# Reordering a fused attention and mixture-of-depths kernel: square sums and PV ahead of the tail scores, transposes between the last two score blocks, gates spread by broadcast weights

## The chip, the core and the metric

The kernel runs on one core of a Trainium2 chip, alone. The metric is the device time of one execution in microseconds. Before the change it was 286.28 us, the median of three (286.19 to 293.61).

## The reference, cut to what matters

Cosine attention over 8 batches, 12 heads, 448 tokens of 64 elements, then a mixture-of-depths block in which the 128 best tokens of each batch pass through a two-layer network:

```python
q_n = q / (norm(q) + 1e-06);  k_n = k / (norm(k) + 1e-06)
attn = softmax(q_n @ k_n.T / tau)          # 448 x 448 for each head
x = attn @ v                               # -> [8, 448, 768]
scores = einsum('bsd,d->bs', x, w_gate)
for b in range(8):
    top_idx = argpartition(-scores[b], 128)[:128]
    h = maximum(x[b, top_idx] @ w1, 0)     # 768 -> 1024
    ye = h @ w2                            # 1024 -> 768
    out[b] = x[b]
    out[b, top_idx] += sigmoid(scores[b, top_idx])[:, None] * ye
```

## The kernel before

The loop runs over 48 pairs of heads, six to a batch. In iteration i, pair i gets its scores and exponentials, pair i - 1 its product with v (PV), pair i + 1 its transposes, pair i + 2 its scaling, and pair i + 6 its squares. 448 tokens are three chunks of 128 and a tail of 64; the tails of both heads of a pair share one block, `scores(i, 3)`. The norms are taken in groups: ScalarE squares, TensorE sums groups of eight with identity weights, VectorE finishes the sum, ScalarE takes the root (`norm_a`), VectorE the reciprocal (`norm_b`). The MoE block of a batch is spread in pieces over the iterations of the next batches; the letters D1, A, C, D3, B, P1 and P2 are the places in an iteration at which such pieces are issued.

```python
# ... pools, loads, constants; ps_sc: two buffers of two PSUM banks, in rotation; ps_t (qkT_ps), ps_o (o_ps), ps_m (m_ps): one buffer each ...
# ... square(p): squares of q and k of pair p on ScalarE; sum_pe(p): 8 matmuls with the identity add them by eights ...
def sum_dve(p, dst):
    n, m = nplace[p]
    nc.vector.tensor_reduce(
        ss_tiles[n][:, m].rearrange("p a b -> p (a b)"),
        dst.rearrange("p (n d) -> p n d", d=D8), axis=AX.X, op=ALU.add)

def norm_a(n):
    gn = NORMS[n][1]
    rs = prep.tile([P, 3, 2, NB7], FP32, name="rs", bufs=3)
    rs_tiles[n] = rs
    nc.scalar.activation(rs[:, :gn], ss_tiles[n][:, :gn], AF.Ln)
    nc.scalar.activation(rs[:, :gn], rs[:, :gn], AF.Exp, scale=0.5)
    nc.scalar.activation(rs[:, :gn], rs[:, :gn], AF.Identity, bias=epsb[:, 0:1])

def norm_b(n):
    gn = NORMS[n][1]
    r = rs_tiles[n][:, :gn].rearrange("p g a b -> p (g a b)")
    nc.vector.reciprocal(r, r)
# ... scale(p): q, k times rs to bf16 (qkn, one buffer) on GpSimd; values(p): v to bf16 on GpSimd;
# transposes(p): 28 PE transposes of qkn into qkT_ps; qkT_copy(p): VectorE copies them to SBUF ...
def scores(i, c, sc=None):
    qkT = qkT_tiles[i]
    if sc is None:
        sc = ps_sc.tile([P, 2, 512], FP32, name="sc")
    sc_tiles[i, c] = sc
    if c < NC:
        for u in range(2):
            r = slice(u * Dh, u * Dh + Dh)
            nc.tensor.matmul(out=sc[:, u, :S],
                             lhsT=qkT[r, KO + c * P:KO + (c + 1) * P],
                             rhs=qkT[r, :S], start=True, stop=True,
                             tile_position=(u * Dh, 0))
    else:
        nc.tensor.matmul(out=sc[:, 0, :S], lhsT=qkT[:, KT:W],
                         rhs=qkT[:, :S], start=True, stop=True)

# ... exps(i, c): exp of block c to bf16 in expS; pv_tails(i), pv(i): 8 + 24 matmuls of expS with vo into o_ps ...
# ... pv_evac(i), VectorE: rden = 1 / the sums in o_ps (L336), then o_ps times rden into x_b or, for the last pair, x_last (L338) ...
# ... store_x(b): DMA x_b -> out; half_x(b): DMA x_b -> xh in bf16; gate, rank_prep, bank, rank_rep: in the diff below;
# rank_count(b, j), pick(b, j): rank by counting and one-hot picks of 128 tokens, VectorE;
# select (8 matmuls), gather (24), ffn1 (2 x 24), ffn2 (2 x 8), scatter: the MoE block of batch b;
# at(slot, where, fn) queues MoE work for an iteration and a place, run(i, where) emits it ...
for i in range(N + 1):
    live, prev, nxt = i < N, i > 0, i + 1 < N
    # ... loads ...
    run(i, "P1")
    sq = SQ.get(i - 1, [])
    scores(i, 0)
    if prev:
        pv_tails(i - 1)
    sc = ps_sc.tile([P, 2, 512], FP32, name="sc")
    scores(i, 3, sc)
    sums(sq, sc)
    exps(i, 0)
    exps(i, 3)
    for p in SQ.get(i, []):
        square(p)
    run(i, "D1")
    sums_dve(sq, sc)
    norms(sq, i, True)
    if prev:
        pv(i - 1)
        pv_evac(i - 1)
    run(i, "A")
    if i < 3:
        warm(8)
    scores(i, 1)
    exps(i, 1)
    scores(i, 2)
    exps(i, 2)
    if nxt:
        transposes(i + 1)
        qkT_copy(i + 1)
    if i + 2 < N:
        scale(i + 2)
        values(i + 2)
    run(i, "P2")
    run(i, "C")
    norms(sq, i, False)
    run(i, "D3")
    if i < 3:
        warm(8)
    run(i, "B")

# ... after the loop: PV of the last pair, the rest of batch 6, all of batch 7 (in the diff) ...
```

## Time and profile before

One profiled execution, span 286.9 us, mean granted TensorE clock 0.957. All times below are from it.

| part of the work | where | each |
|---|---|---|
| exponentials of a full block, 128x896 | L293, ScalarE, 144 times | 914 ns |
| exponentials of a tail block, 128x448 | L296, ScalarE, 48 times | 538 ns |
| squares, 128x896 | L197, ScalarE, 48 times | 945 ns |
| last step of the square sums | L210, VectorE, 48 times | 272 ns |
| gate product of a chunk, 128x768 | L358, VectorE, 28 times | 1103 ns |
| rank by counting, 128x448 | L408, VectorE, 24 times | 677 ns |
| gates on a diagonal, 128x512 | L366, GpSimd, 7 times | 1076 ns |
| gates spread by fp32 product, 128x448 | L396, TensorE, 16 records | 587 ns |
| scaling of q and k, 128x896 | L235, GpSimd, 47 times | 1689 ns |

The profile's page gives the busy time of each engine, the costliest groups of instructions (line, engine, operation, output and inputs, number, busy time, mean of one) and the chain of work that ended last. PE is TensorE's matmuls, PEld its weight loads, DVE is VectorE, ACT ScalarE, POOL GpSimd. The view of waits has, for an engine and a line, what ended its idle time, how long in total, how often, and the longest. In the timeline a row is a start, a duration, the engine, the line and the operation, with the idle time before it in brackets.

57.55 MB are moved in all, 201 GB/s on the mean. Loads of q and k take about 10 us from issue to landing.

### The profile page before, as it was taken

The numbers are of one execution on the slowest core, as the hardware profiler recorded it, in microseconds if no ns is written. First come the engines' busy times: TensorE is split into PE (matmuls) and PEld (weight loads), VectorE is DVE, ScalarE is ACT, GpSimd is POOL, SyncE is SP. The second block draws the span as 40 slices with busy tenths as digits, with TensorE's granted clock in tenths as the row PEclk, the third lists the DMA queues.
The fourth block names the chain that finished last, engine by engine and source line by source line (L and its number), as shares of the span: only waits on it lengthen the run. The fifth ranks groups of instructions, "written<-read, shape, count | busy, mean of one in ns | idle before, by whom it ended". The sixth has DMA issues, their size and how long they took to land.

```text
span 286.9 us, 10402 instructions
## 1 busy us (share of the span) xinstructions
PE 230.8 (80%) x4503; PEld 174.2 (61%) x4503; DVE 181.3 (63%) x482; ACT 208.4 (73%) x322; POOL 150.7 (53%) x183
## 2 busy tenths in 40 slices
PE   7576687788599979997998869987799679859760
PEld 7365565566477657765875548755577457538540
DVE  2313336985776679667875497848866777795620
ACT  3677979999588798888896788869777665573310
POOL 6443465879345674567445747376348463902202
PEclk9997979999789999999799999999999999997997
DMA  7999999999999996999599969998704580549444
GB/s 266 284 252 286 263 263 249 315 276 260 261 309 293 273 193 150 285 273 210 113 247 287 252 112 217 283 270 153 177 21 88 82 194 3 105 61 184 104 55 55
DMA packets 32989, 57.55 MB, mean 201 GB/s; under 512 B 2224, under 2 KB 28784, under 8 KB 32048
## 3 DMA queue, kind: packets, MB, share of 16 engines
q1 hardware_dynamic: 28016, 43.75, 57.8%
q0 software_dynamic: 4512, 12.45, 24.5%
q8 instruction: 35, 0.57, 0.8%
q10 hardware_dynamic: 416, 0.69, 0.7%
q14 instruction: 10, 0.08, 0.1%
HBM read 39.71 MB, written 14.16 MB: 188 GB/s over the span
## 4 chain that ended last, share of the span: by engine, by line
PE 41%; DVE 21%; ACT 16%; DMA 10%; issue 7%; POOL 2%; SPq 1%; POOLq 1%; DVEq 0%; ACTq 0%
ACT expS L293 8%; PE sc L280 8%; DMA qk_raw<-in_k_dram 6%; PE o_ps L320 6%; PE m_ps L483 5%; DVE junk L408 5%; PE qkT_ps L262 5%; DVE junk L358 4%; DMA xh<-x_b 4%; PE sc L204 4%; PE m_ps L475 4%; ACT sq L197 3%; PE m_ps L462 3%; PE sc L285 3%; POOL qkn L235 2%
## 5 line engine op out<-in xcount | busy, mean ns | idle before, releaser
L293 ACT ACTIVATE expS<-sc 128x896 bf16<-128x896 f32 x144 | 126.5, 914 | 37.6 <-PE sc L280 36.8
L235 POOL TENSOR_TENSOR qkn<-qk_raw,rs 128x896 bf16<-128x896 f32 (+1 forms) x48 | 80.7, 1681 | 101.0 <-PE qkT_ps L262 44.0
L280 PE MATMUL sc<-qkT 64*128 64x448 bf16 x288 | 49.3, 368 | 28.8 <-DVE qkT L268 15.6
L197 ACT ACTIVATE sq<-qk_raw 128x896 bf16<-128x896 f32 x48 | 45.1, 945 | 6.0 <-DMA qk_raw<-in_k_dram 4.2
L320 PE MATMUL o_ps<-vo,expS 128*128 128x65 bf16 x1152 | 46.3, 197 | 0.0
L320 PEld LDWEIGHTS <-expS 128*128 128x128 bf16 x1152 | 42.7, 100 | 0.5
L280 PEld LDWEIGHTS <-qkT 64*128 64x128 bf16 x288 | 13.1, 94 | 45.4 <-issue 20.4
L268 DVE COPY qkT<-qkT_ps 128x960 bf16<-128x960 bf16 x48 | 31.4, 655 | 12.5 <-PE qkT_ps L262 12.5
L262 PEld LDWEIGHTS <-qkn 64*64 64x64 bf16 x1344 | 25.4, 111 | 15.8 <-issue 11.0
L338 DVE TENSOR_TENSOR x_b<-o_ps,rden 128x512 f32<-128x512 f32 x47 | 32.5, 691 | 2.3 <-DMA xh<-x_b 0.7
L358 DVE CUSTOM_DVE_ANT_0 junk<-x_b,wg_b 128x768 bf16<-128x768 f32 (+1 forms) x32 | 33.3, 1040 | 0.2
L262 PE MATMUL qkT_ps<-iden_b,qkn 64*64 64x64 bf16 x1344 | 30.8, 196 | 2.1 <-POOL qkn L235 2.1
L242 POOL CAST vo<-v_raw 128x448 bf16<-128x448 f32 x48 | 32.0, 668 | 0.0
L210 DVE TENSOR_REDUCE ss<-sc 128x14 f32<-128x112 f32 x48 | 12.7, 272 | 29.6 <-ACT expS L296 24.5
L296 ACT ACTIVATE expS<-sc 128x448 bf16<-128x448 f32 x48 | 25.8, 538 | 5.1 <-PE sc L204 5.1
L204 PE MATMUL sc<-sq,iden_b 128*128 128x112 bf16 x384 | 28.0, 222 | 0.0
L204 PEld LDWEIGHTS <-iden_b 128*128 128x128 bf16 x384 | 24.7, 103 | 4.9 <-issue 1.3
L475 PEld LDWEIGHTS <-w_sb 128*128 128x128 bf16 x384 | 22.3, 99 | 3.2 <-issue 2.2
L408 DVE SCALAR_TENSOR_TENSOR junk<-m_ps,own,tie 128x448 bf16<-128x448 f32 (+1 forms) x32 | 21.8, 680 | 0.9
L225 DVE RECIPROCAL rs<-rs 128x42 f32<-128x42 f32 (+2 forms) x18 | 7.0, 387 | 22.3 <-ACT rs L220 14.1
L498 POOL DMA_INDIRECT out_dram<-oe,idx x8 | 13.0, 1628 | 14.5 <-DVE oe L448 7.0
L475 PE MATMUL m_ps<-xeT,w_sb 128*128 128x128 bf16 x288 | 18.1, 219 | 1.6 <-DVE xeT L446 1.6
(90 smaller groups left out, 272.6 us busy)
## 6 DMA issues: line engine op xcount, KB each, us to landing
qk_raw<-in_q_dram SPq DMA_DIRECT2D x15, 672.0 KB, 9.8
qk_raw<-in_k_dram SPq DMA_DIRECT2D x15, 672.0 KB, 9.4
v_raw<-in_v_dram SPq DMA_DIRECT2D x30, 192.0 KB, 10.0
out_dram<-x_b SPq DMA_DIRECT2D x7, 768.0 KB
xh<-x_b POOLq DMA_DIRECT2D x7, 768.0 KB, 8.3
v_raw<-in_v_dram SPq DMA_DIRECT2D x30, 144.0 KB, 9.0
out_dram<-x_b SPq DMA_DIRECT2D x7, 576.0 KB, 4.7
w_sb<-in_moe_w_dram POOLq DMA_DIRECT2D x2, 1536.0 KB, 19.8
```

The costliest lines, as they stand in the source:

```text
L197: nc.scalar.activation(sq_tiles[p], raw[gi % NRAW][0][:, :, g].rearrange("p a b d -> p a (b d)"), AF.Square)
L204: nc.tensor.matmul(out=dst, lhsT=iden_b, rhs=sq[:, :, s * D8:(s + 1) * D8], start=(s == 0), stop=(s == Dh // D8 - 1))
L235: eng.tensor_mul(kn[:, :, b0:b1], qk[:, :, g, b0:b1], rs[:, m, :, b0:b1].rearrange("p a (b o) -> p a b o", o=1) .to_broadcast([P, 2, b1 - ...
L242: nc.gpsimd.tensor_copy(vo_bufs[p % NB][:, :, :Dh], raw[gi % NRAW][1][:, g])
L262: nc.tensor.transpose(out=qkT_ps[r, o:o + T], in_=kn[r, a, s], identity=iden_b[r, r], tile_position=(u * T, u * T))
L280: nc.tensor.matmul(out=sc[:, u, :S], lhsT=qkT[r, KO + c * P:KO + (c + 1) * P], rhs=qkT[r, :S], start=True, stop=True, tile_position=(u * D ...
L293: nc.scalar.activation(ex[:, 2 * c:2 * c + 2], sc[:, :, :S], AF.Exp, scale=inv_tau)
L320: nc.tensor.matmul(out=o_ps[:, u, j * E:(j + 1) * E], lhsT=ex[:, 2 * c + u, qc(j)], rhs=vo[:, u * NS + c], start=False, stop=(c == NC - 1) ...
L338: nc.vector.tensor_mul(dst.rearrange("p j (u d) -> p j u d", u=2), o[:, :, :, :Dh], rden.to_broadcast([P, NS, 2, Dh]))
L358: nc.vector.tensor_tensor_reduce(out=junk[:, d0:d1], in0=x_tiles[b][:, j, d0:d1], in1=wg_b[:, d0:d1], scale=1.0, scalar=0.0 if prev is Non ...
L408: nc.vector.scalar_tensor_tensor(out=junk[r], in0=st[b]["rep"][r, :S], scalar=st[b]["own"][r, j:j + 1], in1=tie[r, j, :], op0=ALU.subtract ...
L475: nc.tensor.matmul(out=ps[:, f * CAP:(f + 1) * CAP], lhsT=w1_sb[:, t, fc * P:(fc + 1) * P], rhs=xeT[t], start=(t == 0), stop=(t == KD - 1))
```

## The change

It changes the order within an iteration and does three things besides.

- **Order.** The square sums and the PV product of the pair before go ahead of the tail score block on TensorE; on VectorE the sums go ahead of the gates, with one rank count (the new place D0) in front. The transposes of the next pair go between score blocks 1 and 2, from pair 2 on. The reciprocal of a norm group moves to the next iteration. The purpose is that an engine's queue doesn't stand before a late input while ready work is behind it.
- **Places of the MoE pieces.** Gate products move by an iteration or to D3; the preparation of the ranks goes to a new place, P1b; squares of the first pairs move later; norm groups become aligned with the load groups.
- **Spreading the gates.** Each token's gate has to stand on all partitions. Before, GpSimd put the gates on a diagonal, and a product with ones in fp32 spread them. After, the gate is split into three bf16 parts (these existed already for the selection), and each part's column, broadcast to 128 columns, is the weight operand of a product with the identity: 15 small products in place of two fp32 ones.
- **The tail.** The score buffers are closed after the loop and four one-bank tiles opened in their place. The last batch's gates are reduced chunk by chunk, the last chunk's on GpSimd and ScalarE, the spreading is issued in the middle of an ffn1, and ffn1 and ffn2 are cut in two so that they can start on the first half of their input.

```diff
@@ -78,7 +79,7 @@
     starts = {g0: gi for gi, (g0, gn) in enumerate(GROUPS)}
     place = {g0 + g: (gi, g) for gi, (g0, gn) in enumerate(GROUPS) for g in range(gn)}
-    NORMS = [(0, 1), (1, 2), (3, 2)]
+    NORMS = [(0, 1), (1, 2), (3, 2), (5, 1)]
     while sum(NORMS[-1]) < N:
         NORMS.append((sum(NORMS[-1]), min(3, N - sum(NORMS[-1]))))
     nplace = {g0 + g: (n, g) for n, (g0, gn) in enumerate(NORMS) for g in range(gn)}
# ... iden_f, ones_f, iden_x and their fills: removed; ps_sc: opened last, so that it can be closed ...
@@ -351,53 +343,49 @@
# ... gate(b, j, d0, d1, prev, dst): sum of x * w_gate over columns d0 to d1 on VectorE (L358); gets x as another source ...
-    def rank_prep(b, split=False):
+    def rank_prep(b, eng=None):
         g = gates[b % 2]
-        diag = moe.tile([P, NS, P], FP32, name="diag", bufs=1)
-        nc.gpsimd.tensor_mul(
-            diag[:, :2 if split else NS], iden_x[:, :2 if split else NS],
-            g[:, :2 if split else NS].rearrange("p (j o) -> p j o", o=1)
-            .to_broadcast([P, 2 if split else NS, P]))
-        if split:
-            for j in (2, 3):
-                nc.scalar.activation(diag[:, j], iden_x[:, j], AF.Copy,
-                                     scale=g[:, j:j + 1])
+        eng = eng or nc.gpsimd
         sg = moe.tile([P, NS, 3], BF16, name="sg")
         r1 = moe.tile([P, NS], FP32, name="r1")
-        nc.gpsimd.tensor_copy(sg[:, :, 0], g)
-        nc.gpsimd.tensor_sub(r1, g, sg[:, :, 0])
-        nc.gpsimd.tensor_copy(sg[:, :, 1], r1)
-        nc.gpsimd.tensor_sub(r1, r1, sg[:, :, 1])
-        nc.gpsimd.tensor_copy(sg[:, :, 2], r1)
-        st[b].update(diag=diag, sg=sg)
+        eng.tensor_copy(sg[:, :, 0], g)
+        eng.tensor_sub(r1, g, sg[:, :, 0])
+        eng.tensor_copy(sg[:, :, 1], r1)
+        eng.tensor_sub(sg[:, :, 2], r1, sg[:, :, 1])
+        st[b]["sg"] = sg
     wide = []
     def bank(big=False):
         if not big:
             return ps_m.tile([P, 512], FP32, name="m_ps")
-        if not wide:
-            t = ps_sc.tile([P, 2, 512], FP32, name="sc")
-            wide.extend((t[:, 1], t[:, 0]))
-        return wide.pop()
+        return wide[0].tile([P, 512], FP32, name="w_ps")
     def rank_rep(b):
-        g, diag = gates[b % 2], st[b]["diag"]
+        sg = st[b]["sg"]
         rep = bank()
-        nc.tensor.matmul(out=rep[:, :S], lhsT=ones_f,
-                         rhs=diag.rearrange("p j c -> p (j c)")[:, :S],
-                         start=True, stop=True)
-        nc.tensor.matmul(out=rep[:, S:S + NS], lhsT=iden_f, rhs=g,
-                         start=True, stop=True)
+        for j in range(NS):
+            c0, n = (j * P, P) if j < NC else (SM, T)
+            for e in range(3):
+                nc.tensor.matmul(out=rep[:, c0:c0 + n],
+                                 lhsT=sg[:, j, e:e + 1].to_broadcast([P, P]),
+                                 rhs=iden_b[:, P - n:], start=(e == 0), stop=(e == 2))
+        for e in range(3):
+            nc.tensor.matmul(out=rep[:, S:S + NS], lhsT=iden_b, rhs=sg[:, :, e],
+                             start=(e == 0), stop=(e == 2))
         own = moe.tile([P, NS], FP32, name="own")
         nc.vector.tensor_copy(own, rep[:, S:S + NS])
         st[b].update(rep=rep, own=own)
@@ -464,17 +452,23 @@
                                  start=(j == 0), stop=(j == NS - 1))
         evac(eng, xe.rearrange("p t c -> p (t c)"), ps[:, :(t1 - t0) * CAP], AF.Copy)
-    def ffn1(b, part, eng="D", big=False):
+    def ffn1(b, part, eng="D", big=False, cut=0, between=None):
         xeT = st[b]["xeT"]
         h = moe.tile([P, 4, CAP], BF16, name=f"hT{part}")
         st[b].setdefault("hT", []).extend(h[:, t] for t in range(4))
         ps = bank(big)
-        for f in range(4):
+        order = [(f, t) for t0, t1 in ((0, cut), (cut, KD)) for f in range(4)
+                 for t in range(t0, t1)]
+        for m, (f, t) in enumerate(order):
             fc = part * 4 + f
-            for t in range(KD):
-                nc.tensor.matmul(out=ps[:, f * CAP:(f + 1) * CAP],
-                                 lhsT=w1_sb[:, t, fc * P:(fc + 1) * P],
-                                 rhs=xeT[t], start=(t == 0), stop=(t == KD - 1))
+            if between and m == len(order) // 2:
+                between()
+            nc.tensor.matmul(out=ps[:, f * CAP:(f + 1) * CAP],
+                             lhsT=w1_sb[:, t, fc * P:(fc + 1) * P],
+                             rhs=xeT[t], start=(m == 0) if cut else (t == 0),
+                             stop=(t == KD - 1), skip_group_check=bool(cut))
         evac(eng, h.rearrange("p t c -> p (t c)"), ps, AF.Relu)
     def ffn2_mm(b, n, ps, t0, t1):
@@ -511,28 +505,30 @@
             fn(*args)
-    late = dict(gate=(1, 2, 3, 4), rep=5, half=5, rank=6, select=7,
-                ffn=((8, "B"), (9, "B"), (10, "B"), (11, "A")))
+    late = dict(gate=((2, "D1"), (3, "D1"), (4, "D1"), (5, "D1")), rep=5, half=5, rank=6,
+                select=7, ffn=((8, "B"), (9, "B"), (10, "B"), (11, "A")))
     mid = dict(late, ffn=((8, "B"), (9, "A"), (9, "B"), (10, "A")))
-    early = dict(gate=(1, 1, 2, 3), rep=4, half=4, rank=5, select=6,
-                 ffn=((7, "B"), (8, "A"), (8, "B"), (9, "A")))
-    last = dict(gate=(1, 1, 2, 2), rep=3, half=3, rank=4, select=5, ffn=())
+    early = dict(gate=((2, "D1"), (3, "D1"), (3, "D3"), (4, "D1")), rep=4, half=4, rank=5,
+                 select=6, ffn=((7, "B"), (8, "A"), (8, "B"), (9, "A")))
+    last = dict(gate=((1, "D1"), (2, "D1"), (2, "D3"), (3, "D1")), rep=3, half=3, rank=4,
+                select=5, ffn=())
     for b in range(B - 1):
         s = HP * (b + 1)
         m = last if b == B - 2 else early if b == B - 3 else mid if b == B - 4 else late
         for j in range(NS):
-            at(s + m["gate"][j], "D1", gate, b, j)
-        at(s + m["gate"][3], "P2", rank_prep, b)
+            d, w = m["gate"][j]
+            at(s + d, w, gate, b, j)
+        at(s + m["gate"][3][0], "P1b", rank_prep, b)
         at(s + m["half"], "P1", half_x, b)
         at(s + m["rep"], "B", rank_rep, b)
         for j in range(NS):
-            at(s + m["rank"], "D1" if j < 2 else "D3", rank_count, b, j)
+            at(s + m["rank"], ("D0", "D1", "D3", "D3")[j], rank_count, b, j)
         for j in range(NS):
             at(s + m["rank"], "D3", pick, b, j)
         at(s + m["select"], "A", select, b)
         at(s + m["select"], "C", select_b, b)
-        at(s + m["select"], "B", gather, b, 0)
+        at(s + m["select"], "B", gather, b, 0, "A" if b == B - 2 else "D")
         if b < B - 2:
             at(s + m["select"] + 1, "A", gather, b, 1)
         for (d, w), (fn, n) in zip(m["ffn"], ((ffn1, 0), (ffn1, 1), (ffn2, 0), (ffn2, 1))):
@@ -541,12 +537,10 @@
                 at(s + d, "P2", scatter, b)
     bb = B - 1
     ga = const.tile([P, NS], FP32)
-    gb = const.tile([P, NS], FP32)
     gc = const.tile([P, NS], FP32)
     for j in range(NS):
-        at(N - 3, "D1", gate, bb, j, 0, 2 * P, None, ga)
-        at(N - 1, "D1", gate, bb, j, 2 * P, 4 * P, ga, gb)
-        at(N - 1, "D3", gate, bb, j, 4 * P, 5 * P, gb, gc)
+        at(N - 3, "D3", gate, bb, j, 0, 2 * P, None, ga)
+        at(N - 1, "D3", gate, bb, j, 2 * P, 5 * P, ga, gc)
     at(N - 1, "P2", half_x, bb, 5 * P)
     at(N - 1, "P2", store_x, bb, None, 0, 5 * P)
     at(3, "D1", load_wg)
@@ -555,7 +549,7 @@
     SQ = {}
     for p in range(3, N):
-        SQ.setdefault({3: 0, 4: 0, 5: 1, 6: 1, 7: 2, 8: 2}.get(p, p - 6), []).append(p)
+        SQ.setdefault({3: 0, 4: 0, 5: 1, 6: 2, 7: 2, 8: 3}.get(p, p - 6), []).append(p)
     SW = 2 * NB7 * D8
     wps = bank()
@@ -573,12 +567,17 @@
         for m, p in enumerate(ps):
             sum_dve(p, sc[:, 1, m * SW:(m + 1) * SW])
-    def norms(ps, i=None, early=None):
+    due = []
+    def norms(ps, i=None):
         for p in ps:
             n, g = nplace[p]
-            if g == NORMS[n][1] - 1 and (i is None or early == (NORMS[n][0] == i + 2)):
+            if g == NORMS[n][1] - 1:
                 norm_a(n)
-                norm_b(n)
+                if i is None or NORMS[n][0] == i + 2:
+                    norm_b(n)
+                else:
+                    due.append(n)
     warm(30)
     for n in (0, 1):
@@ -613,27 +612,35 @@
         scores(i, 0)
         if prev:
             pv_tails(i - 1)
-        sc = ps_sc.tile([P, 2, 512], FP32, name="sc")
-        scores(i, 3, sc)
-        sums(sq, sc)
         exps(i, 0)
-        exps(i, 3)
         for p in SQ.get(i, []):
             square(p)
+        run(i, "D0")
+        sc = ps_sc.tile([P, 2, 512], FP32, name="sc")
+        sums(sq, sc)
+        sums_dve(sq, sc)
+        while due:
+            norm_b(due.pop())
+        first = [p for p in sq if NORMS[nplace[p][0]][0] == i + 2]
+        norms(first, i)
         run(i, "D1")
-        sums_dve(sq, sc)
-        norms(sq, i, True)
+        run(i, "P1b")
         if prev:
             pv(i - 1)
             pv_evac(i - 1)
         run(i, "A")
         if i < 3:
             warm(8)
+        scores(i, 3, sc)
+        exps(i, 3)
         scores(i, 1)
         exps(i, 1)
+        if i > 1 and nxt:
+            transposes(i + 1)
+            qkT_copy(i + 1)
         scores(i, 2)
         exps(i, 2)
-        if nxt:
+        if i < 2:
             transposes(i + 1)
             qkT_copy(i + 1)
         if i + 2 < N:
# ... norms(sq, i, False) becomes norms([p for p in sq if p not in first], i) ...
@@ -650,38 +657,42 @@
     b = B - 2
+    sc_pool.close()
+    wide.append(sc_pool.enter_context(tc.tile_pool(name="ps_w", bufs=4, space=PSUM)))
     pv_tails(N - 1)
     pv(N - 1)
     pv_evac(N - 1)
     gather(b, 1, "A", True)
     store_x(bb, x_last, 5 * P, D)
-    xg = moe.tile([P, NS, P], FP32, name="xg", bufs=1)
-    nc.vector.tensor_mul(
-        xg, x_last,
-        wg_b[:, 5 * P:D].rearrange("p (o d) -> p o d", o=1).to_broadcast([P, NS, P]))
-    gd = moe.tile([P, NS], FP32, name="gd", bufs=1)
-    nc.vector.tensor_reduce(gd, xg, axis=AX.X, op=ALU.add)
-    nc.vector.tensor_add(gates[bb % 2], gd, gc)
+    g7 = gates[bb % 2]
+    xg = moe.tile([P, P], FP32, name="xg", bufs=1)
+    nc.gpsimd.tensor_mul(xg, x_last[:, NC], wg_b[:, 5 * P:D])
+    for j in range(NC):
+        gate(bb, j, 5 * P, D, gc, g7, x_last)
+    xgs = moe.tile([P, P], FP32, name="xgs", bufs=1)
+    gd = moe.tile([P, 1], FP32, name="gd", bufs=1)
+    nc.scalar.activation(xgs, xg, AF.Copy, accum_out=gd)
+    nc.vector.tensor_add(g7[:, NC:], gd, gc[:, NC:])
     ffn1(b, 0, "A", True)
-    rank_prep(bb, True)
-    ffn1(b, 1, "A", True)
+    rank_prep(bb, nc.vector)
     nc.scalar.activation(xh_last, x_last, AF.Copy)
-    rank_rep(bb)
+    ffn1(b, 1, "A", True, 0, lambda: rank_rep(bb))
     ffn2(b, 0, "A", True)
     ffn2(b, 1, "A", True)
     for j in range(NS):
         rank_count(bb, j)
         pick(bb, j)
     scatter(b)
-    gather(bb, 0, "A", True, 3)
-    gather(bb, 1, "D", True, 3)
+    gather(bb, 0, "A", True)
+    gather(bb, 1, "D", True)
     select(bb)
     select_b(bb)
-    ffn1(bb, 0, "A", True)
+    ffn1(bb, 0, "A", True, 4)
     ffn1(bb, 1, "D", True)
     ps = [bank(True), bank(True)]
-    ffn2_mm(bb, 0, ps[0], 0, KF)
-    ffn2_mm(bb, 1, ps[1], 0, KF)
+    for t0, t1 in ((0, KF // 2), (KF // 2, KF)):
+        for n in range(2):
+            ffn2_mm(bb, n, ps[n], t0, t1)
     ffn2_evac(bb, 0, ps[0], "A")
     ffn2_evac(bb, 1, ps[1], "D")
     scatter(bb)
```

## The prediction

> **What bounds the kernel now.** I read the page first, then the busy time by stretches of the span, then the waits, then the timeline of a few pairs of heads (the loop's iterations, counted from 0), and last the chain of work that ended last. The page's busy times name no single engine:
>
> ```profile
> PE 230.8 (80%) x4503; PEld 174.2 (61%) x4503; DVE 181.3 (63%) x482; ACT 208.4 (73%) x322; POOL 150.7 (53%) x183
> ```
>
> The stretches (columns: stretch, its length, then PE, PEld, DVE, ACT, POOL busy us with counts, granted clock, DMA share, GB/s) show three regimes:
>
> ```profile
> 35.00:60.00 25.00, 19.32 (x424) 14.12 (x426) 16.23 (x33) 23.03 (x35) 17.50 (x16) 0.93 1.09 277
> 120.00:150.00 30.00, 28.15 (x561) 21.42 (x560) 22.48 (x58) 25.21 (x39) 17.70 (x21) 0.94 0.92 215
> 235.00:258.00 23.00, 17.73 (x326) 12.61 (x326) 18.63 (x55) 13.03 (x19) 11.36 (x15) 1.00 0.36 66
> ```
>
> Early, ScalarE is full and the DMA runs at its highest rate. In the middle TensorE is full, ScalarE next to full. Late, VectorE is busiest (81%). The waits say what ends the gaps:
>
> ```profile
> ACT expS L293 <- PE sc L280: 36.8, 46, 2.2
> DVE ss L210 <- ACT expS L296: 24.5, 14, 3.4
> PE sc L280 <- DVE qkT L268: 15.6, 14, 3.5
> DVE rs L225 <- ACT rs L220: 14.1, 11, 3.5
> PE sc L280 <- DVE ss L210: 7.2, 12, 0.9
> ```
>
> ScalarE waits for score blocks; TensorE's score blocks wait for VectorE's copy of q/k and its square sums; and VectorE itself stands still in front of an operation whose input is late, with ready work behind it. One iteration in which that happens (timeline, pair 19):
>
> ```profile
> 108.38 0.95 DVE L358 CUSTOM_DVE_ANT_0 junk<-x_b,wg_b 128x768 bf16<-128x768 f32 x1
> ...
> 109.37 0.28 DVE L210 TENSOR_REDUCE ss<-sc 128x14 f32<-128x112 f32 x1
> 109.56 0.20 DVE L336 RECIPROCAL rden<-o_ps 128x8 f32<-128x8 f32 x1
> 109.70 0.37 PE L280 MATMUL sc<-qkT 64*128 64x448 bf16 x2 [0.60 <-DVE ss L210]
> ```
>
> The gate product (L358) stands ahead of the square sum, so the buffer that block 2 needs comes free 1 us late.
>
> The end, from the chain:
>
> ```profile
> 254.77 0.48 DVE junk L358
> 255.30 0.48 DVE junk L358
> 255.83 0.48 DVE junk L358
> 256.63 0.57 issue
> 257.59 12.10 DMA xh<-x_b
> 269.73 1.53 PE sc L462 x24
> ```
>
> The last batch's gate products hold back the PV evacuation of pair 46, which holds back the bf16 copy of x, for which the last gather waits.
>
> **What the Trainium skill says.** "PSUM — Partial Sum Buffer", Engine vs sequencer instructions: the queues of ScalarE, VectorE and GpSimd are strict FIFO. The trace agrees: above, ready sums stand 1 us behind a gate. The same page, PSUM bank collisions raise a hardware error: two engines' accesses to one bank must be kept apart, so guard by bank. Here L210 starts right after L296 although they read different banks of one tile: the wait goes by tile, which is coarser; one-bank tiles in the tail follow from that. "TensorE: Matmul & The Clock Gate", What's actually happening: the clock halves after a window of about 3.4 us with little work. The granted clock was 0.73 in 70 to 80 us, where TensorE waited, so filling gaps may pay twice. "Perfetto Trace Analysis", Identifying the Most-Contended Engine: matmul busy share is a bad measure of headroom; so I add up starts, not busy times.
>
> **The change part by part.** First the floor of an iteration. The starts of the tail exponentials (L296) are 3.82 and 3.86 us apart where nothing else runs, 4.45 with a norm group, one in three: ScalarE needs (2 x 3.84 + 4.45)/3 = 4.04. TensorE went from 121.32 to 125.70 without a gap, 1.40 of it half an ffn2: 2.98 without MoE. Start to start, the MoE pieces are rep 1.07, select about 0.5, gather 0.99 + 0.54, each ffn1 half 1.44, each ffn2 half 1.40. So the six iterations of a batch cost at least: rank 4.04 (ScalarE), select 2.98 + 1.49 = 4.47, 2.98 + 0.54 + 1.44 = 4.96, 4.42, 4.38, 2.98 + 1.40 + 1.07 = 5.45, in all 27.7; pairs 36 to 41, where two batches overlap, 4.04 + 4.47 + 4.96 + 5.82 + 5.45 + 4.04 = 28.8. Measured between the starts 70.91, 103.13, 132.46, 164.45, 195.02, 226.27: 32.2, 29.3, 32.0, 30.6, 31.3, sum 155.4 against 4 x 27.7 + 28.8 = 139.6. 15.8 us are lost. 2.7 of them are a wait for q/k data at 74 us, and about 4 is half clock (6.8 and 3.4 us granted at 0.5, not all on the path). About 9 is VectorE's order, and this the change attacks:
>
> - Sums before the gates, gates one iteration later (away from select): the 7.2 us of TensorE behind ss and 2.6 behind the picks go.
> - Transposes before score block 2: qkT is copied while ScalarE still has two blocks; of the 15.6 us about 5 lie in iterations where TensorE sets the pace.
> - The second half of the norm moved to the next iteration: VectorE no longer stands before ScalarE's norm (14.1 us, mostly off the path).
> - Against it: the tail scores come after PV and slot A. ScalarE has exp (0.84) and square (0.84) to do, while TensorE does sums 0.4, PV 0.92, scores 0.2 and 0.2 of latency: 1.7 against 1.7, so about 0.15 lost per iteration where ScalarE sets the pace, 0.5 where squares are over: 1 us in all.
>
> I take two thirds of the 9, 6 us. rank_rep: two fp32 products (1.07) become 15 small ones; at the gather's 62 ns (0.99/16) 0.93: 0.14 x 7 = 1 us, within the 6. GpSimd loses 1.04 us of diag a batch, off the path.
>
> Pairs 42 to 46 took 253.56 - 226.27 = 27.3. No squares are left, so TensorE's 2.98 becomes 2.55: with select and gather 4.04, with gather and ffn1 4.53, with ffn1 and ffn2 5.39, with ffn2 and rep 5.02, and the last 3.1 by ScalarE: 22.1. Of 5.2 lost, I take half: 2.5, since the same gates still have to run on a busy VectorE.
>
> The tail: exponentials ended at 256.73, PV of the last pair started at 258.45, x_last was there at 261.0. With the gates behind pv_evac the gather's bank is free sooner and PV starts at once: 0.3 + 1.0 + 0.9 = 2.3 after the exponentials, instead of 4.3: 2.0 us. From x_last to the last pick took 8.75 (269.75): gate 1.7, diag 1.85, rep with its copy 1.4, four count-and-picks 3.8. New, counted from x_last: three gates of 0.35 + 0.08 and an add of 0.16 make 1.45 (the fourth runs on GpSimd and ScalarE beside them); the split in four small VectorE steps of 0.14, as L428 to L432 take, ends at 2.0; TensorE does the rest of the gather, waits 0.6 for its copy, and is through one and a half ffn1 halves at 2.4, so rep runs from 2.4 to 3.4; copy 0.25, counts 3.8: 7.5. But ffn2 of the batch before follows the rest of ffn1 (4.1) and its copy (0.8) with 2.76 and ends at about 7.7: 1.0 gained. From there the output went in 9.2; ffn1 starting on four parts and ffn2 on the first half of h give 0.6, as 0.78 us of waiting for the second half of h ends. Sum 3.6; xh, landing 12 us after an issue that moves with the rest, may take 0.3 back.
>
> The start: square 6 no longer blocks ScalarE until 20.6 us; some 3 us there. But from 20 to 80 us the DMA moves 259 to 306 GB/s (stretches of 10 us), and pair 12 waits for q/k until 74.13. I count 0.5.
>
> Sum: 6 + 2.5 + 3.3 + 0.5 - 1 = 11.3; 286.3 - 11.3 = 275.0. I put it at 275.5.
>
> **Rivals.** *The DMA sets the pace.* For: pair 12's wait, and a share of 0.92 in the middle. Against: the rate there is 215 GB/s, with 282 reached in 60 to 90; at 28.8 us a batch 215 x 31.1/28.8 = 232 is needed. If it binds, only pairs 42 on and the tail gain: 280. *TensorE alone sets the pace.* For: 28.15 of 30 us busy; then reordering finds nothing in the middle but 1 us of rep: 279.5. Against: the 5.3 to 6.6 us iterations, of which only two lie in half clock. *The late tail scores starve ScalarE.* With an ffn2 half in slot A, block 3 comes 1.4 us later; if block 2 then waits for it, each batch loses about 1 us in two iterations: 10 us back, 285. Against: those iterations are TensorE's, and block 1 and the transposes stand between. *All works, and the clock holds too:* the 15.8 less 2.7, plus 4 late and 3.5: 266.
>
> **Range and chances.** The sizes of the middle and of pairs 42 to 46 are the uncertain terms: from a third to all of it is -4.5 to +6 us around 275.5. Range 269 to 282. 2% is 280.6: faster 0.80, within 0.15, slower 0.05.
>
> **What would show it.** Right: L280's waits for ss and for sel are gone, and that for qkT is below 6 us; L225 waits less for L220; L296 waits more (5.1 now) for L285; batches of 28.5 to 29.5 us; x_last 2.3 us after the last exponential. Wrong: new waits of squares or qkn for DMA, L293 still waiting some 35 us, a longer chain through xh, or iterations with ffn in slot A over 5.6 us.

## The result and the profile after

The changed kernel takes 277.14 us (median of four runs, 275.43 to 279.67), beside 287.21 us (median of four, 286.19 to 293.61) for the kernel before. The ratio is 0.964, its 95% interval 0.955 to 0.973: 10 us less. 275.5 was predicted, within 269 to 282.

The total came out 1.6 us from the prediction, but its terms did not. The table follows the start of the tail exponentials of single pairs (L296 before, L288 after) through the two profiled executions, 286.9 and 277.9 us long. Executions of one kernel come shorter and longer, and every ratio here compares the shorter ones alone (it is not the quotient of two medians), while five profiles are of longer ones: those of the changed kernel (277.9 us; its other executions took 273.6 to 275.9), of the old order put back (both runs), of w2 at pair 11 in the kernel before, and of the last version. Another execution of the changed kernel, of 276.4 us, shows the same stages within 1.3 us.

| stage | before | after | gained | predicted |
|---|---|---|---|---|
| start of the span to pair 6 | 46.64 | 44.12 | +2.5 | |
| start to pair 13 | 78.06 | 81.80 | -3.7 | +0.5 |
| pair 13 to 42 | 148.21 | 140.72 | +7.5 | +5.0 (6 - 1) |
| pair 42 to 47 | 27.29 | 26.34 | +1.0 | +2.5 |
| pair 47 to the end | 33.34 | 29.04 | +4.3 | +3.3 |
| sum | 286.9 | 277.9 | +9.0 | +11.3 |

The tail exponentials come later within an iteration in the new order than in the old, which shifts these stages. By the start of a pair's first exponentials the four gains are -3.0 (start to pair 13), +8.5, +0.7 and +2.7; from the end of the last exponentials to the end of the span it took 30.1 us before and 26.8 after, 3.3 less.

The page's busy times of the changed kernel hardly differ from those before for the busy engines: TensorE has 2 us more, VectorE 3.5 us less. (GpSimd has 15 us less.) The work is nearly the same; there are fewer gaps.

```profile
PE 232.8 (84%) x4591; PEld 175.2 (63%) x4591; DVE 177.8 (64%) x480; ACT 207.1 (75%) x323; POOL 135.7 (49%) x160
```

Its waits (engine and line, what it waited for, us in all, times, longest):

```profile
DVE ss L202 <- PE sc L196: 33.7, 28, 6.9
ACT expS L288 <- PE sc L277: 17.2, 19, 1.9
ACT expS L285 <- PE sc L272: 16.3, 21, 2.4
PE sc L272 <- ACT expS L288: 11.6, 7, 7.2
ACT sq L189 <- DMA qk_raw<-in_k_dram: 10.0, 3, 7.4
DVE gr L427 <- ACT gr L426: 9.1, 8, 2.2
PE sc L272 <- DVE qkT L260: 8.0, 12, 3.0
DVE rs L217 <- ACT rs L212: 3.6, 4, 0.9
```

ScalarE's wait for full score blocks fell from 36.8 to 16.3 us. VectorE's wait for the tail exponentials (24.5) is gone: ss now waits for its own sums instead, with gates behind it that nothing waits for yet. TensorE's waits for ss (7.2) and for sel (2.6) are gone; that for qkT fell from 15.6 to 8.0. Two lines are new or larger. A square stands 7.4 us before k data, and one score block stands 7.2 us behind the exponentials that come after this square, which is the same stall seen from TensorE. And VectorE waits for ScalarE in front of gr, up to 2.2 us. Of the wait of tail blocks (L288 for L277), 10 of the 17.2 us fall into the eight iterations with half an ffn1 or ffn2 ahead of the tail scores.

The busy time by stretches (columns as before):

```profile
70.00:80.00 10.00, 2.55 (x35) 1.81 (x31) 2.88 (x10) 4.03 (x8) 2.19 (x2) 0.67 1.07 254
120.00:150.00 30.00, 26.54 (x559) 19.85 (x552) 21.42 (x55) 24.19 (x38) 16.15 (x18) 1.00 0.93 226
228.00:250.00 22.00, 17.87 (x328) 12.23 (x328) 18.96 (x48) 12.22 (x17) 10.90 (x13) 0.94 0.44 82
```

In the second TensorE has done as many products as before (559, 561), at the full granted clock instead of 0.94. Between pairs 13 and 42, 6.8 us were granted half clock before (up to 81.5, and 3.4 us from 136.1 on) and 1.9 us after (up to 83.7). As an estimate from the difference of 4.9 us, at most 2.5 us of what the middle gained is clock; the runs don't separate it. The stretch holds one gap of 1.85 us at 123.2 in the middle of a PV, of which the profile says only "issue". In the last VectorE is still the busiest (86%). In the first, no engine works much while the DMA share is highest: pair 12 waits for k. ScalarE's timeline there, first one line of before, then after:

```profile
74.13 0.95 ACT L197 ACTIVATE sq<-qk_raw 128x896 bf16<-128x896 f32 x1 [2.69 <-DMA qk_raw<-in_k_dram]
```

```profile
67.59 0.92 ACT L285 ACTIVATE expS<-sc 128x896 bf16<-128x896 f32 x1 [0.28 <-PE sc L272]
75.90 0.95 ACT L189 ACTIVATE sq<-qk_raw 128x896 bf16<-128x896 f32 x1 [7.39 <-DMA qk_raw<-in_k_dram]
```

The same square stood 2.7 us before the change. Its k was issued at 56.05 (before: 55.89) and landed 19.8 us later. The loads of q and k issued between 33 and 57 us all took 19 to 21 us, those from 80 us on 4 to 15. The wait is 4.7 us longer for two reasons: ScalarE reaches the square 2.9 us earlier than before (at 68.51 instead of 71.44), and the square starts 1.8 us later (75.90 instead of 74.13), since the data come later. Only the second is a loss against the kernel before; the first is gain that the wait takes back. In the middle the batches, from pair 12 on, take 29.3, 30.6, 27.6, 29.2 and 29.0 us, where they took 32.2, 29.3, 32.0, 30.6 and 31.3.

### The profile page after: what moved, and what is told of

It reads as the page before. It is cut to its first block, busy times and chain, and to the rows that moved or that the text cites. A ratio compares the mean times of both kernels' runs of the same rounds, so it can differ in the third digit from the quotient of the medians.

```text
span 277.9 us, 10534 instructions
## 1 busy us (share of the span) xinstructions
PE 232.8 (84%) x4591; PEld 175.2 (63%) x4591; DVE 177.8 (64%) x480; ACT 207.1 (75%) x323; POOL 135.7 (49%) x160
## 4 chain that ended last, share of the span: by engine, by line
PE 38%; DMA 24%; ACT 16%; DVE 13%; issue 4%; SPq 3%; POOLq 1%; DVEq 0%; ACTq 0%
DMA qk_raw<-in_k_dram 17%; ACT expS L285 8%; PE m_ps L468 6%; PE sc L272 6%; PE m_ps L477 5%; PE o_ps L312 5%; DVE junk L351 5%; PE qkT_ps L254 4%; DMA qk_raw<-in_q_dram 4%; PE sc L196 3%; ACT sq L189 3%; DMA v_raw<-in_v_dram 3%; ACT expS L288 2%; DVE junk L396 2%; SPq L108 2%
## 5 line engine op out<-in xcount | busy, mean ns | idle before, releaser
L285 ACT ACTIVATE expS<-sc 128x896 bf16<-128x896 f32 x144 | 126.3, 917 | 16.9 <-PE sc L272 16.3
L272 PE MATMUL sc<-qkT 64*128 64x448 bf16 x288 | 53.7, 368 | 22.7 <-ACT expS L288 11.6
L272 PEld LDWEIGHTS <-qkT 64*128 64x128 bf16 x288 | 14.8, 93 | 46.0 <-issue 30.0
L312 PEld LDWEIGHTS <-expS 128*128 128x128 bf16 x1152 | 42.1, 100 | 2.6 <-issue 2.2
L260 DVE COPY qkT<-qkT_ps 128x960 bf16<-128x960 bf16 x48 | 31.3, 652 | 13.0 <-PE qkT_ps L254 12.0
L288 ACT ACTIVATE expS<-sc 128x448 bf16<-128x448 f32 x48 | 25.9, 539 | 17.4 <-PE sc L277 17.2
L254 PE MATMUL qkT_ps<-iden_b,qkn 64*64 64x64 bf16 x1344 | 31.4, 195 | 3.7 <-issue 2.1
L351 DVE CUSTOM_DVE_ANT_0 junk<-x_b,wg_b 128x768 bf16<-128x768 f32 (+1 forms) x32 | 31.4, 980 | 0.1
L234 POOL CAST vo<-v_raw 128x448 bf16<-128x448 f32 x48 | 28.9, 604 | 0.0
L196 PEld LDWEIGHTS <-iden_b 128*128 128x128 bf16 x384 | 22.4, 102 | 5.2 <-issue 2.0
L477 PE MATMUL m_ps<-w_sb,hT 128*128 128x384 bf16 x96 | 17.6, 326 | 0.3 <-DVE oe L436 0.3
## 6 DMA issues: line engine op xcount, KB each, us to landing
w_sb<-in_moe_w_dram POOLq DMA_DIRECT2D x2, 1536.0 KB, 20.6
```

Of the source, the lines that this page charges most:

```text
L196: nc.tensor.matmul(out=dst, lhsT=iden_b, rhs=sq[:, :, s * D8:(s + 1) * D8], start=(s == 0), stop=(s == Dh // D8 - 1))
L254: nc.tensor.transpose(out=qkT_ps[r, o:o + T], in_=kn[r, a, s], identity=iden_b[r, r], tile_position=(u * T, u * T))
L272: nc.tensor.matmul(out=sc[:, u, :S], lhsT=qkT[r, KO + c * P:KO + (c + 1) * P], rhs=qkT[r, :S], start=True, stop=True, tile_position=(u * D ...
L285: nc.scalar.activation(ex[:, 2 * c:2 * c + 2], sc[:, :, :S], AF.Exp, scale=inv_tau)
L288: nc.scalar.activation(ex[:, TAIL], sc[:, 0, :S], AF.Exp, scale=inv_tau)
L312: nc.tensor.matmul(out=o_ps[:, u, j * E:(j + 1) * E], lhsT=ex[:, 2 * c + u, qc(j)], rhs=vo[:, u * NS + c], start=False, stop=(c == NC - 1) ...
```

## The experiments

The kernels below are the changed kernel with one edit, unless another start is named. Ratios are to the kernel before on the same chip. Its median there was 288.6 us for the changed kernel again, w2 at pair 10 in both kernels and the old order; 291.2 for w2 at pair 11 and for gates, spreading and tail put back; 290.6 for the other four. The chips differ between these groups and the changed kernel was repeated in the first alone, so comparisons across groups go by ratios.

That "pair n took" some time means from the tail exponentials of pair n - 1 to those of pair n. The wait for k above falls into pair 12 in the new order and into pair 13 in the old one, where the square comes behind the tail exponentials. The expectations call it the wait of square 18, since pair 18's square is due there.

### What holds up pair 12

The second of the two MoE weight loads, w2 (1536 KB as written, issued by GpSimd at 47.73, some 20.6 us to landing), shares the DMA with the late k load. First the changed kernel as it is, as the mark for the others of its group:

> The changed kernel again, as the mark for the three others: 277 us, ratio 0.964. Square 18 waits for its q and k (7.4 us in the first profile); if that wait hangs on the moment it should vary by some us from run to run.

It took 278.89 us, ratio 0.969 (0.953 to 0.985), with 6.9 us of waiting at the same square and 11.13 us for pair 12: the wait hardly varied between these two profiles. Then w2 later, at pair 10, and the same in the kernel before:

```diff
-    at(6, "P2", load_w, w2_sb, moe_w2, kn[:, 1, 0, 0:1])
+    at(10, "P2", load_w, w2_sb, moe_w2, kn[:, 1, 0, 0:1])
```

> The load of w2 (3.1 MB) moved from pair 6 to pair 10. Theory, the full DMA takes the early gain: q and k of pairs 18 to 20 land about 6 us earlier, the wait of square 18 falls from 7.4 us to under 2, TensorE's clock stays whole there, and the time falls by about 4 us to 273 (0.950). Rival, the wait only lends the loads a lead that the middle uses up later: the waits move on to pairs 15 to 24 (w2 then competes there) and the time stays within 1 us of 277.

> The same move in the kernel before. Theory: its wait of 2.7 us goes and the time falls by 2 to 3 us, to 284; that is less than in the changed kernel, since the old order reached pair 12 later and so lost less there. Rival, the loss comes from the new order of ScalarE (square ahead of the tail exponentials) and not from the bytes: the kernel before doesn't change (within 1 us).

Both lost: 287.68 us, ratio 0.9987 (0.995 to 1.002), and 300.81 us, ratio 1.045 (1.035 to 1.055); neither expectation foresaw it. The wait at that square was all but gone (4.64 us for pair 12 in the new order, 4.43 for pair 13 in the old), but pair 14 took 21.35 and 19.94 us. The waits of the changed kernel with w2 at pair 10, between 70 and 110 us:

```profile
DVE x_b L330 <- issue: 15.5, 1, 15.5
PE m_ps L450 <- DVE pks L418: 15.2, 1, 15.2
PEld L450 <- DMA xh<-x_b: 14.6, 1, 14.6
```

The gather (L450) names VectorE's picks, but its weight load tells the cause: xh, the bf16 copy of batch 0's x. GpSimd issued w2 at 63.64 and xh at 64.60, both into its one queue, and xh took 25.2 us to land, where the median of such copies is 10.5:

```profile
63.64 0.96 POOL L174 DMA_DIRECT2D w_sb<-in_moe_w_dram  x1 [0.32 <-POOL w_sb L173]
64.60 0.56 POOL L344 DMA_DIRECT2D xh<-x_b  x1
...
DMA to landing us min/median/max: 5.6/10.5/25.2
```

"DMA: Bandwidth & Descriptors" of the Trainium skill, Queues, rings and completion order, says that a DMA engine alternates between the queues that have work, packet by packet. From this one would infer that a small transfer shares with a large one in another queue, but stands behind one in its own. This run shows the second half: 768 KB stood behind 1536 KB issued 1 us earlier. Up to 78 us the large packets in this queue are all of w2's size (1536 bytes); most of xh's (6144 bytes) follow between 80 and 88 us. So w2 went one pair further, behind xh:

```diff
-    at(6, "P2", load_w, w2_sb, moe_w2, kn[:, 1, 0, 0:1])
+    at(11, "P2", load_w, w2_sb, moe_w2, kn[:, 1, 0, 0:1])
```

> The changed kernel with the load of w2 at pair 11 instead of 6, behind the copy of x to bf16 (xh) of batch 0 in GpSimd's DMA queue, not ahead of it as at pair 10. Theory, the full DMA takes the early gain: the wait of square 18 falls from 7 us to under 1, the gather of batch 0 (pair 13) doesn't wait for xh, the first ffn2 (pair 16, some 90 us) waits at most 2 us for w2: 273 us, ratio about 0.95, 5 us under the changed kernel. Rival, bytes are bytes: w2 then delays the loads for pairs 21 to 23 and the wait reappears at pair 15: 278.

273.01 us, ratio 0.942 (0.930 to 0.953). Pair 12 took 4.11 us instead of 11.6, pair 13 6.41 instead of 5.04, and no square waits for k (one waits 1.9 us for q). Pair 13 starts at 75.40: 2.7 us ahead of the kernel before instead of 3.7 behind. The theory was right: between two and three per cent of the time had been lost to the place of one load. The kernel before, with the same edit:

> The kernel before with w2 at pair 11. Theory, the old order was late enough at pair 12 to lose only 2.7 us to the DMA: 2 to 4 us less than before, ratio 0.99; so the move is worth 5 us in the changed kernel and about half of it in the old one. Rival, the move helps the same in both: 0.98 or less.

287.0 us, ratio 0.998 (0.992 to 1.004): nothing, less than the theory and its rival said. Its profile is of an execution of 292.04 us, the longest of 21, so what it shows need not hold for the others. In it pair 13 took 4.83 us instead of 7.15, but pair 14 took 10.20 instead of 5.49: there the gather stands for xh, 2.9 us by this line of its waits, and TensorE came back at half clock (16 gather products took 1.86 us). Here xh was issued 3.3 us ahead of w2 and still took 12.2 us to land, so a place ahead in the queue doesn't protect it fully.

```profile
PEld L462 <- DMA xh<-x_b: 2.9, 1, 2.9
```

So with w2 at pair 11 in both kernels the whole change is worth 0.9977 - 0.9417 = 5.6%, 16 us. The move gains in the new order and not in the old one; whether another place would have gained in the old one wasn't tried.

### Which part of the change does the work

The order within an iteration, undone alone:

```diff
         scores(i, 0)
         if prev:
             pv_tails(i - 1)
+        sc = ps_sc.tile([P, 2, 512], FP32, name="sc")
+        scores(i, 3, sc)
+        sums(sq, sc)
         exps(i, 0)
+        exps(i, 3)
 # ... the sums, norms and gates in their former order; scores(i, 3), exps(i, 3) after PV: removed ...
-        if i > 1 and nxt:
-            transposes(i + 1)
-            qkT_copy(i + 1)
         scores(i, 2)
         exps(i, 2)
-        if i < 2:
+        if nxt:
             transposes(i + 1)
             qkT_copy(i + 1)
```

> The changed kernel with the loop's old order: tail scores first, sums after the gates, transposes last, reciprocal of the norm at once; gates, spreading and tail stay new. Theory, the order is what gains in the middle: pairs 13 to 41 lose some 5 of the 7.5 us gained, the waits of score blocks for ss and for qkT come back, 283 us (0.985), though the wait at pair 12 shrinks by some us. Rival, the gates' new places and the spreading carry the middle: within 1.5 us of 277.

287.92 us, ratio 0.9925 (0.988 to 0.998). From pair 13 to 41 its profile has 147.6 us, the changed kernel's second profile 134.9, the kernel before 143.5. The loss is larger than the theory said (0.985). The waits of exponentials for score blocks and of score blocks for qkT are back:

```profile
ACT expS L285 <- PE sc L272: 45.1, 45, 3.4
...
PE sc L272 <- DVE qkT L260: 15.1, 15, 3.1
```

The same with w2 at pair 11, where no DMA stall mixes in:

> The run of 273 us with the loop's old order (gates, spreading and tail stay new): what the order is worth where the DMA doesn't bound. Theory: with the wait at pair 12 gone the order's gain is no longer cut: 11 us more than 273, 284 (0.98). Rival, part of the 9 us that the old order cost with the stall is the stall's lead (loads run ahead during it): 6 us more, 279.

284.48 us, ratio 0.980 (0.977 to 0.983), beside 0.942 with the new order: 3.8%, 11 us, as the theory said. Of the 16 us, then, 11 hang on the order, and 5 are what the rest brings with the old order. Of the order, the transposes alone were put back behind block 2:

```diff
-        if i > 1 and nxt:
+        if False and nxt:
             transposes(i + 1)
             qkT_copy(i + 1)
         scores(i, 2)
         exps(i, 2)
-        if i < 2:
+        if nxt:
             transposes(i + 1)
             qkT_copy(i + 1)
```

> The run of 273 us with only the transposes back behind score block 2. Theory: they decide how soon the next pair's first block can start where ScalarE or VectorE sets the pace (rank and select pairs, two of six), about 0.4 us each: 3 us more, 276 (0.95). Rival, TensorE works through in nearly all pairs, so the place doesn't matter: under 1 us.

287.77 us, ratio 0.992 (0.989 to 0.996): 5%, some 14.7 us, more than undoing all of the order. Neither expectation is near it. Its waits:

```profile
PE sc L272 <- ACT expS L288: 20.9, 47, 1.7
...
PE sc L272 <- DVE qkT L260: 9.1, 10, 2.8
```

With the transposes in their new place (w2 at pair 11) the same two lines are:

```profile
PE sc L272 <- DVE qkT L260: 8.9, 13, 3.0
...
PE sc L272 <- ACT expS L288: 3.5, 5, 1.7
```

The wait for qkT, for which the transposes were thought to move, is 9.1 us with them last and 8.9 with them between: no difference. The other went from 3.5 us in 5 waits to 20.9 in 47, one in nearly every pair. TensorE's timeline of one iteration with the transposes last:

```profile
131.45 0.35 PE L277 MATMUL sc<-qkT 128*128 128x448 bf16 x1
131.73 0.36 PE L272 MATMUL sc<-qkT 64*128 64x448 bf16 x2
132.43 0.37 PE L272 MATMUL sc<-qkT 64*128 64x448 bf16 x2 [0.34 <-ACT expS L288]
132.73 0.63 PE L254 MATMUL qkT_ps<-iden_b,qkn 64*64 64x64 bf16 x28
```

and one of the kernel with w2 at pair 11, transposes between:

```profile
137.19 0.35 PE L277 MATMUL sc<-qkT 128*128 128x448 bf16 x1
137.47 0.36 PE L272 MATMUL sc<-qkT 64*128 64x448 bf16 x2
137.76 0.63 PE L254 MATMUL qkT_ps<-iden_b,qkn 64*64 64x64 bf16 x28
138.32 0.36 PE L272 MATMUL sc<-qkT 64*128 64x448 bf16 x2
```

There are two score buffers. The tail scores (L277) fill one, block 1 the other, so block 2 needs the tail's, which its exponentials free. In the old order the tail came early and its buffer was long free. In the new order its exponentials have only begun when block 2 is due, and TensorE would stand. The 28 transposes fill just that gap; placed behind block 2 they start as much later, and with them all that waits for them (qkT's copy waits 39.4 us for transposes here, 12.3 with them between). So "sums and PV first" opens a wait, and "transposes between" closes it: without the second, the new order is slower than the old (0.992 against 0.980). The transposes between, with all else in the old order, weren't run. That the buffer is the cause is read from these waits and places; a third score buffer wasn't tried.

The places of the gates and counts, put back alone (w2 as in the changed kernel):

```diff
-    late = dict(gate=((2, "D1"), (3, "D1"), (4, "D1"), (5, "D1")), rep=5, half=5, rank=6,
+    late = dict(gate=(1, 2, 3, 4), rep=5, half=5, rank=6,
 # ... early and last likewise; all gates at D1 ...
-            at(s + m["rank"], ("D0", "D1", "D3", "D3")[j], rank_count, b, j)
+            at(s + m["rank"], "D1" if j < 2 else "D3", rank_count, b, j)
```

> The changed kernel with the gates and rank counts back in their old places (an iteration earlier, so that one falls into the select iteration; two counts in D1; the last batch's in D1). Theory, places matter less than the order: 2 to 3 us more than the changed kernel, half of it in pairs 42 to 47, where D1 stands ahead of pv_evac: 281 (0.978). Rival, the places are what gains: 5 us or more, 284.

284.14 us, ratio 0.977 (0.967 to 0.988), and 141.3 us from pair 13 to 41 instead of 134.9: by these two profiles the places are worth 6.4 us there, so the rival was nearer. The whole times say less, since the ratio's interval overlaps that of the changed kernel (0.953 to 0.985). The worths of order and places don't add up: each was measured with the other in place, and together they exceed what the middle gained. The spreading of the gates by a diagonal and fp32 products, put back alone in the loop:

```diff
+            nc.gpsimd.tensor_mul(
+                diag, iden_x, g.rearrange("p (j o) -> p j o", o=1).to_broadcast([P, NS, P]))
...
+            nc.tensor.matmul(out=rep[:, :S], lhsT=ones_f,
+                             rhs=st[b]["diag"].rearrange("p j c -> p (j c)")[:, :S],
+                             start=True, stop=True)
```

> The changed kernel with the loop's gates spread by the diagonal and the fp32 product again (the tail keeps the new way). By the two profiles rep takes TensorE 1.07 before and about 0.75 after, so 7 x 0.3 = 2 us at most; GpSimd gets 1.04 us a batch more, off the path. Theory: 1 to 2 us more, 280. Rival, rep is in the one iteration that is fullest (ffn2 and rep), and VectorE's count waits for it as well: 3 to 4 us.

283.41 us, ratio 0.978 (0.969 to 0.987), 0.9% over the changed kernel's 0.969, with overlapping intervals: a loss isn't certain. Of the profiles' difference of 5.6 us, 2.5 stand before pair 13 (1.7 of it in pair 9, at a wait for k that comes before the first diagonal is made, so not from the products), 2.8 between pairs 13 and 42. The fp32 pieces start 1.07 us before the next work on TensorE (1.04 in one batch); the bf16 pieces 0.75 in four of these five batches and 1.51 in the fifth, where a gap of 0.60 us, called "issue" by the profile, stands among them. That makes 0.8 of these 2.8. The rest, with GpSimd's 1.03 us for each diagonal as a candidate, isn't settled.

The code after the loop, put back alone (score buffers kept open, gates of the last columns in one product and one reduction, whole gathers and ffn halves in sequence):

```diff
-    sc_pool.close()
-    wide.append(sc_pool.enter_context(tc.tile_pool(name="ps_w", bufs=4, space=PSUM)))
...
-    for j in range(NC):
-        gate(bb, j, 5 * P, D, gc, g7, x_last)
+    nc.vector.tensor_reduce(gd, xg, axis=AX.X, op=ALU.add)
...
-    gather(bb, 0, "A", True)
+    gather(bb, 0, "A", True, 3)
```

> The changed kernel with the tail as before: two-bank tiles, gates of the last 128 columns by one product and one reduction on VectorE, spreading behind ffn1, no cut in ffn1 and ffn2. The prediction gave the tail 3.6 us, of which 2.0 come from the loop's last pair and not from the tail's code; so 1.6 us more: 280.5. Rival, the xh copy ends last anyway (it landed about 12 us after its issue before): within 0.5 us.

279.96 us, ratio 0.964 (0.952 to 0.976), which can't be told from the changed kernel's. By the profiles, pair 47 to the end took 30.7 us instead of 28.9: the new code is worth 1.8 there, by one pair of profiles. The other 2.5 of the 4.3 in the table are not the work of this code.

### The last pairs, and a last version

Pair 46 to 47 took 6.97 us in the changed kernel, 3.97 before. VectorE's timeline after the loop shows a related hold-up, reciprocal of gr ahead of the gates ahead of x_last:

```profile
251.52 0.17 DVE L427 RECIPROCAL gr<-gr 128x1 f32<-128x1 f32 x1 [2.16 <-ACT gr L426]
251.60 0.60 DVE L351 CUSTOM_DVE_ANT_0 junk<-x_b,wg_b,ga 128x384 bf16<-128x384 f32 x1
...
253.57 0.62 DVE L351 CUSTOM_DVE_ANT_0 junk<-x_b,wg_b,ga 128x384 bf16<-128x384 f32 x1
...
254.35 0.69 DVE L330 TENSOR_TENSOR x_last<-o_ps,rden 128x512 f32<-128x512 f32 x1
```

VectorE stood 2.16 us for two small ScalarE steps that wait behind exponentials, with four gates behind them whose inputs were there. So the reciprocal moved behind later work, the first partial gates of the last batch behind the picks of pair 46, and w2 to pair 11:

```diff
+    def select_c(b):
+        gr = st[b]["gr"]
 # ... the reciprocal and what follows it, one iteration later; for the last batch after ffn1's issue ...
-        at(N - 3, "D3", gate, bb, j, 0, 2 * P, None, ga)
+        at(N - 2, "D3", gate, bb, j, 0, 2 * P, None, ga)
```

> w2 behind xh, as in the run of 273 us; besides, the reciprocal of the selected gates (which VectorE holds 9.1 us in all for ScalarE, 2.2 of it in the last pair ahead of the last gates) goes to the next pair, in the last pair behind the gates; and the first gate products of the last batch go behind the picks of pair 46. Theory, VectorE's order also bounds the last pairs: pair 47 starts its scores 2.4 us earlier and x_last comes some 2.5 us earlier, the rest of the loop gains under 1: 270 us, 0.932. Rival, VectorE is simply full there (86% in 228 to 250 us): the same work in another order gives under 1 us.

271.83 us, ratio 0.934 (0.923 to 0.945): faster than the kernel before and, by the intervals, than the changed kernel (0.955 to 0.973). Pair 46 to 47 took 4.25 us. VectorE there has the gates ahead of the reciprocal:

```profile
245.43 0.62 DVE L351 CUSTOM_DVE_ANT_0 junk<-x_b,wg_b,ga 128x384 bf16<-128x384 f32 x1
...
246.64 0.16 DVE L430 RECIPROCAL gr<-gr 128x1 f32<-128x1 f32 x1
```

From the tail exponentials of pair 46 to x_last complete it needs 10.1 us, the changed kernel 13.2 (13.2 also with w2 alone moved). But its interval overlaps that of w2 alone (0.930 to 0.953), so a gain over w2 alone is not shown. Its profile (of an execution of 273.56 us) is 3.2 us behind that of w2 alone at pair 46, 0.6 of it before pair 12 (pairs 13, 17 and 35 took 7.4, 7.2 and 7.3 us instead of 6.4, 6.1 and 6.5, the rest is spread). Whether the later reciprocal causes that is open. From x_last to the end it took 24.1 us instead of 22.7. There the last gather stands for xh, which took 11.3 us to land; with w2 alone this wait isn't there:

```profile
PEld L453 <- DMA xh<-x_b: 1.6, 1, 1.6
```

So once VectorE's order in the last pairs is mended, this copy is the next limit in that profile.

## Why the prediction held, and where its steps did not

The main mechanism was right: VectorE's order and the order of the score blocks cost about 9 us in the middle, and reordering gained 7.5 and 8.7 us there in two profiles, some of it perhaps clock. One reason given for it, that of the transposes, was wrong. Most of the signs named for it are there (no wait for ss or sel; rs waits 3.6 us instead of 14.1; ScalarE's wait at the tail block up from 5.1 to 17.2; three of five batches at 29.0 to 29.3, within 28.5 to 29.5). Others are not: qkT is waited for 8.0 us instead of under 6, a square waits for DMA, and iterations with half an ffn ahead of the tail scores take 5.6 to 6.5 us, over the 5.6 named. Those cost little against before, where the same pieces took 5.3 to 6.6. Two of its sums are not as written: 0.3 + 1.0 + 0.9 is 2.2 and not 2.3, and "from a third to all" of the two uncertain terms is 3.8 us less gain to 5.7 more, not 4.5 and 6. Neither matters beside the range. Step by step:

- **"Square 6 no longer blocks ScalarE ... I count 0.5" failed**: -3.7. The gain was there, 2.5 us by pair 6 (1.3 in the second profile), and was lost again at pair 12. The prediction saw both the full DMA and the wait of pair 12, and made them a rival ("the DMA sets the pace") for the middle, where it was wrong; it was right for the stretch before pair 13. The step asked how much the wait would keep of the gain, not whether the changed traffic would make it longer. With w2 five pairs later the start gives +2.7 and the total 273.0.
- **"I take two thirds of the 9, 6 us" and "1 us in all" for the late tail scores**: 7.5 instead of 5.0 net (8.7 by the second profile), so the share of two thirds was too small or the cost of the late tail scores too large; that cost was not measured by itself.
- **"rank_rep: 0.14 x 7"** was right in sum and mis-sized in detail. In the middle 1.07 became 0.75 in four batches, 0.32 gained instead of 0.14, and 1.51 in the fifth, 0.44 lost with the "issue" gap; that gap stands in the profile with w2 moved too. It makes 0.8 for the five, where 0.7 was said. The 62 ns for each product came from the gather; these 15, three of them with 4 columns and three with 64, took 50 on the mean without the gap.
- **"Transposes before score block 2 ... of the 15.6 us about 5" failed as a reason.** The wait for qkT halved, but it stays where it is when the transposes go back. Their worth, 14.7 us, is that they stand where TensorE would wait for the tail's buffer. The rival "the late tail scores starve ScalarE" had "block 1 and the transposes stand between" as its counter-argument. That was right, and it was the argument on which the whole change rests: without the transposes there, the kernel is slower than with the old order (0.992 against 0.980).
- **"Pairs 42 to 46: I take half, 2.5"**: 1.0. Up to pair 46 it was 4.0, more than said; pair 47 lost 3.0 (by first exponentials 2.5 and 1.7). The four partial gates of the last batch stand on VectorE ahead of the counts, the x_b evacuation and the qkT copy of the last pair. At 246.02 TensorE had stood 3.02 us for that copy; soon after it ran at half clock.
- **"2.3 after the exponentials" failed**: 3.96 (251.08 to 255.04), where 4.27 was before. VectorE was still in the gates behind gr. That TensorE ran at half clock there (16 gather products took 1.89 us, PV 1.84) is not the cause: with w2 moved they took 1.07 and 1.24, and x_last came 3.97 after the last exponential all the same. In the last version, with these gates ahead of gr, it is 3.71, and VectorE works without a gap. 0.3 us was gained of 2.0.
- **The rest of the tail** made it up. From x_last to the last pick 7.23 us (7.5 predicted, 7.7 with the ffn2 beside it; 8.75 before); from there to the end of VectorE's last oe 7.74 (9.21 before: 1.5 gained, 0.6 predicted); the exponentials of the last pair end 2.22 us after its tail block starts instead of 3.17. 0.3 + 1.5 + 1.5 + 0.95 = 4.3, but the 0.95 is only the shift of the mark within the pair. Without it the tail gained the 3.3 that was predicted, from other parts than predicted.

So the start came out 4.2 below its term and the late pairs 1.5, the middle 2.5 and the tail 1.0 above (by first exponentials 3.5 and 1.8 below, the middle 3.5 above and the tail 0.6 below). That these partly cancel is luck, and a reason why the total lies so near.

## What to carry to other kernels

When a reordering lets an in-order engine run ahead, list what each buffer it needs next is freed by, and put independent work of about that length between: here 28 transposes of 0.56 us in one place or the next decided over 5% of the time. Before counting an early gain, look at the first wait for data after it and at the large loads in flight there; moving one load cost 3% at one place and gained 2 to 3% at the next, and a load issued 1 us ahead of a small urgent copy in the same queue held that copy up by some 15 us. A small step that waits for a second engine, such as the reciprocal of gr, goes behind the work that is ready: with the gates moved as well, x_last came 3.0 us sooner after pair 46, though a gain in the whole time isn't shown.

## What the runs showed of the hardware

VectorE's gate product (two inputs from SBUF) took 0.95 us alone and up to 2.04 beside GpSimd's scaling of q and k. The timeline of the changed kernel:

```profile
233.74 1.69 POOL L227 TENSOR_TENSOR qkn<-qk_raw,rs 128x896 bf16<-128x896 f32 x1 [3.77 <-PE qkT_ps L254]
234.20 2.04 DVE L351 CUSTOM_DVE_ANT_0 junk<-x_b,wg_b 128x768 bf16<-128x768 f32 x1
...
239.42 1.69 POOL L227 TENSOR_TENSOR qkn<-qk_raw,rs 128x896 bf16<-128x896 f32 x1 [0.69 <-PE qkT_ps L254]
239.95 1.44 DVE L351 CUSTOM_DVE_ANT_0 junk<-x_b,wg_b 128x256 bf16<-128x256 f32 x1
```

GpSimd's products end at 235.43 and 241.11; the gates end at 236.24 and 241.39, about their own length (0.95 and 0.42) after that. "SBUF — State Buffer" of the Trainium skill, SBUF: two separate sides, describes this: an exclusive port that a VectorE operation with two SBUF inputs and a GpSimd operation reading SBUF take in turn, the later one blocked for the whole instruction. The trace agrees within 0.15 us. In this profile two of the 28 full gates and one partial gate met a scaling that had begun before them, and each took about 1 us longer. In the last version the four partial gates of this kind stand elsewhere and took 0.41 to 0.42; since other things changed as well, what these meetings cost the kernel is open.

TensorE's broadcast products (L383) take one column of the split gates, repeated 128 times, as weights; their weight loads took 98 ns, as those of the gather do with 128 different columns.
